# Seven block products instead of eight in both FFN products of the last six token chunks, with a new exchange of the turned probabilities and one load of queries and keys

## Chip, cores and metric

One core of one Trainium2 chip. The metric is the device time of one execution in microseconds (us); a kernel's time is the median of its runs.

## What is computed

Block-causal attention for 8 batches of 8 heads (576 positions, head dimension 64, blocks of 64 positions), then on its output, taken as 4608 tokens of 512 features, a feed-forward network (FFN) of two products with a leaky ReLU between them:

```python
scores = (1.0 / np.sqrt(D)) * np.matmul(q, k.transpose(0, 1, 3, 2))
scores = np.where(block_i >= block_j, scores, -1000000000.0)
attn = np.exp(scores - np.max(scores, axis=-1, keepdims=True))
attn = attn / (np.sum(attn, axis=-1, keepdims=True) + 1e-09)
attn_out = np.matmul(attn, v).astype(np.float32)
x = np.ascontiguousarray(attn_out.transpose(0, 2, 1, 3)).reshape(B * S, H * D)
h = x @ w_in                       # 4608 x 512 by 512 x 2048
g = np.maximum(0.01 * h, h)
return (g @ w_out).astype(np.float32)   # 4608 x 2048 by 2048 x 512
```

## The kernel before

Every operation is handed to a planner (class `Plan`, line 69) with a cost, a rank and the keys that it reads and writes. Before anything is issued the planner plays all five engines forward with its own costs and writes out one fixed order for each engine; on the chip each engine works through its list and waits by semaphores. A binary operation from SBUF on VectorE is marked "DVE+" (line 298): the planner never lets it run at the same time as an operation on GpSimd.

**FFN.** The tokens are cut into 18 chunks of 256 (`CH`). Every float32 operand is split into a high and a low part, and each product is the sum of three: high by high, high by low, low by high. A chunk has eight steps u. `ffn1` (line 845) makes two blocks of 128 rows of h from the chunk's x (`xh`, `xl`) in 24 matmuls of 256 columns (line 856); ScalarE applies the leaky ReLU (`g`, line 871), ScalarE or VectorE rounds it (`gh`), GpSimd as a rule subtracts (`gl`). `ffn2` (line 876) multiplies both blocks of g by `w_out` in 12 matmuls of 512 columns (line 883) into `p_o`, which collects over the eight steps; then ScalarE copies it to `ob` and it is stored. One chunk is 192 matmuls of 256 columns and 96 of 512. The core of both:

```python
terms = [((wih, wil)[w], x, d) for d in range(ND) for w, x in sides]
nc.tensor.matmul(p_h[z][:, i, :], w[:, d, f * P : (f + 1) * P], (xl if x else xh[y])[:, d, :], ...)
terms = [(a, w, i) for a, w in ((gh[z], woh), (gh[z], wol), (gl[z], woh)) for i in range(2)]
nc.tensor.matmul(p_o[m], a[:, i, m * P : (m + 1) * P], w[:, 2 * u + i, :], ...)
```

There is one `xl`: the low part of a chunk's x is written (`split_x`, line 821) when the chunk before has no first product left.

**Attention.** Heads 0 to 13 go one way. Heads 14 to 63 load queries and keys twice, into both halves of the partitions of `qk_in`, as one tile for query and key (line 509); both are scaled or rounded and their low parts subtracted (lines 511 to 521). After the softmax, VectorE transposes 32 x 32 squares of the probabilities (`turn`, line 749), and four DMAs write them to DRAM (`way`, line 774) and four read them back with their blocks exchanged (`ptm`, line 785); the product with the values reads `ptm` (line 680). The heads are spread over the FFN work of earlier batches; when the last head is done, only FFN chunks are left.

Of the kernel before, what the change touches and what calls it, by code (L numbers as in the profile page):

```python
# [9 lines left out]
F32 = mybir.dt.float32  # L10
# [26 lines left out]
RL = -2.566  # L37
RP = 4.143
RB = 0.5
RT = 2.976  # L40
RV = 0.818
RX = -0.204
RN = -1.299
RF = 4.338
PACE = [5.0, 5.0, 5.67, 5.0, 5.0, 5.0, 5.0, 5.0, 5.0, 5.0, 5.0, 5.0, 5.0, 5.0, 5.0, 5.0, 6.28, 5.0]
TWO = True
RM = -22.489

LEAD = 10.827
LAG = 1.995  # L50
RS = -17.449
RG = -4.487
OFF1 = 3.447
# [4 lines left out]
    "raw": (2200, 675), "first": (3300, 675), "v0": (1600, 900), "k": (900, 1170), "q": (500, 1110), "qk": (1500, 1325), "v": (450, 792),  # L58
    "way": (590, 385), "back": (1090, 1095), "out": (690, 354), "xs": (900, 400), "xin": (1500, 1100),
}  # L60
PADD = 2701.103
HOLD = 277.504
# [5 lines left out]
PAD = 595.177  # L68
PADO = 51.657
SPARE = 42.026  # L70
# [3 lines left out]
    [-0.34, -2.01, -1.04, -0.21, -0.2],  # L74
# [6 lines left out]
    [-0.3, 11.3, 1.53, -0.3, 0.55],  # L81
# [171 lines left out]

def act(n, sb=False):
    return n / 1.2 + (92 if sb else 52)
# [11 lines left out]
def attention_ffn(ctx: ExitStack, tc: tile.TileContext, q2: bass.AP, k2: bass.AP, qk: bass.AP, v: bass.AP, w_in: bass.AP, w_out: bass.AP, out: bass.AP):  # L267
# [38 lines left out]
    const = ctx.enter_context(tc.tile_pool(name="const", bufs=1))  # L306
    psum = ctx.enter_context(tc.tile_pool(name="psum", bufs=1, space=PSUM))
# [20 lines left out]
    way = fixed([4, P, 32 * slots], F32, "way", 2, dram)  # L328
# [13 lines left out]
    rows(0, const)  # L342
    qk_in = fixed([P, 2, S], F32, "qk_in")
# [7 lines left out]
    xr = fixed([P, ND, S], F32, "xr")  # L351
    xs = fixed([P, S], F32, "xs", 2)
    xin = fixed([P, ND, CH], F32, "xin")
    xt = [None] + fixed([ND, P, S], F32, "xt", B - 1, dram)
# [15 lines left out]
    g = fixed([P, 2, CH], F32, "g")  # L370
    gh = fixed([P, 2, CH], F32R, "gh", 2)
    gl = fixed([P, 2, CH], F32R, "gl", 2)
    xh = [fixed([P, ND, CH], F32R, "xh0")]
    xl = fixed([P, ND, CH], F32R, "xl")
    ob = fixed([P, DM], F32, "ob")

    early, coded = ExitStack(), ExitStack()
# [14 lines left out]
    def second_stage():  # L392
        coded.close()
        pool = ctx.enter_context(tc.tile_pool(name="late", bufs=1, side="right", reuse_waits="tile"))
        later["qs"] = fixed([P, S], F32R, "qs", 2, pool)
        later["ks"] = fixed([P, 2, S], F32R, "ks", None, pool)

    def third_stage():
        early.close()
        pool = ctx.enter_context(tc.tile_pool(name="last", bufs=1, reuse_waits="tile"))  # L400
# [580 lines left out]
```

## Time and profile before

| | |
|---|---|
| median of 3 runs (lowest, highest) | 1084.79 us (1084.07, 1092.26) |
| the profiled execution: its own time | 1086.14 us |
| its span, first to last instruction | 1084.4 us |

The difference of 1.7 us between the profiled execution's time and its span lies around the span. In the profile PE is TensorE's matmuls, DVE VectorE, ACT ScalarE, POOL GpSimd, SP the queue that issues all DMAs. A busy time counts a matmul from its issue until its results are out, and these overlap, so how fast TensorE works is read from the distance of starts.

### The profile page before, as it was taken

To read this page: it belongs to the slowest core of one execution; us is meant where nothing else is said; L and a number is where in the kernel's file an instruction comes from. 1 tells how busy PE (TensorE), PEld (TensorE's weight loads), DVE (VectorE), ACT (ScalarE), POOL (GpSimd) and SP (SyncE) were. 2 spreads that over 40 slices of the span, in tenths; PEclk is the share of its full clock that TensorE was granted. 3 is DMA by queue.
4 is the path that set the end of the run, shared out by engine and by line. 5 is a ranking of instruction groups with operands and counts; after the bars stand their busy time and mean duration, and the time that the engine had idled before them with its cause. 6 is when DMAs were issued, how large, how long until landed. Compare 5 with 4: busy or idle time off the path is not lost.

```text
span 1084.4 us, 19280 instructions
## 1 busy us (share of the span) xinstructions
PE 1055.5 (97%) x7048; PEld 913.8 (84%) x7048; DVE 562.5 (52%) x1564; ACT 525.8 (48%) x1297; POOL 326.2 (30%) x315
## 2 busy tenths in 40 slices
PE   7889999989999999999999999999999999999998
PEld 5658889878888889888888888888999999999997
DVE  7989878777787778676778776830000000000000
ACT  7787655655665556565555645632222222222222
POOL 3443334332332233323333332222222222222221
PEclk9989999999999999999999999999999999999999
DMA  7555427888999999887989979980101101001000
GB/s 208 176 173 158 150 97 222 240 255 244 304 247 258 270 250 299 249 248 229 266 245 259 297 229 270 268 222 21 41 5 36 39 1 40 20 20 40 1 21 20
DMA packets 107294, 179.86 MB, mean 166 GB/s; under 512 B 11968, under 2 KB 88768, under 8 KB 107200
## 3 DMA queue, kind: packets, MB, share of 16 engines
q1 hardware_dynamic: 107200, 178.63, 57.0%
q8 instruction: 56, 0.92, 0.4%
q14 instruction: 38, 0.31, 0.1%
HBM read 115.02 MB, written 63.57 MB: 165 GB/s over the span
## 4 chain that ended last, share of the span: by engine, by line
PE 73%; DMA 15%; DVE 5%; ACT 3%; issue 2%; SPq 1%; POOL 0%; ACTq 0%; POOLq 0%; DVEq 0%
PE p_o L883 29%; PE p_h L856 29%; DMA qk_in<-in_qk 8%; PE p_v L680 4%; DMA ptm<-way 3%; PE p_s L530 3%; PE p_v L541 2%; PE p_s L541 2%; PE p_v L636 1%; DMA way<-turn 1%; ACT prow L571 1%; DMA out<-ob 1%; DVE turn L760 1%; DVE nmrec L562 1%; PE p_v L724 1%
## 5 line engine op out<-in xcount | busy, mean ns | idle before, releaser
L298 POOL TENSOR_TENSOR gl<-g,gh 128x512 fp32r<-128x512 f32 x137 | 180.8, 1320 | 461.3 <-ACT gh L283 363.8
L856 PE MATMUL p_h<-xh,wih 128*128 128x256 f32 x1152 | 317.0, 280 | 0.0
L856 PE MATMUL p_h<-xh,wil 128*128 128x256 f32 x1152 | 314.5, 278 | 0.0
L856 PE MATMUL p_h<-xl,wih 128*128 128x256 f32 x1152 | 299.6, 278 | 0.0
L856 PEld LDWEIGHTS p_h<-xh,wih 128*128 128x128 f32 x1152 | 217.1, 188 | 9.5 <-issue 0.8
L871 ACT ACTIVATE g<-p_h 128x512 f32<-128x512 f32 x144 | 85.7, 595 | 281.3 <-PE p_h L856 276.8
L856 PEld LDWEIGHTS p_h<-xh,wil 128*128 128x128 f32 x1152 | 217.2, 189 | 0.6
L856 PEld LDWEIGHTS p_h<-xl,wih 128*128 128x128 f32 x1152 | 208.3, 189 | 8.4
L883 PE MATMUL p_o<-woh,gh 128*128 128x512 f32 x576 | 180.3, 394 | 1.4 <-ACT ob L283 1.2
L883 PE MATMUL p_o<-woh,gl 128*128 128x512 f32 x576 | 179.4, 393 | 0.2 <-POOL gl L298 0.2
L883 PE MATMUL p_o<-wol,gh 128*128 128x512 f32 x576 | 179.0, 392 | 0.0
L297 DVE TENSOR_TENSOR xl<-xin,xh 128x1024 fp32r<-128x1024 f32 (+3 forms) x21 | 19.5, 942 | 259.0 <-PE p_h L856 259.0
L760 DVE STREAM_TRANSPOSE turn<-prow 128x128 f32<-128x128 f32 (+3 forms) x400 | 144.4, 397 | 17.7 <-POOL prow L601 12.1
L883 PEld LDWEIGHTS p_o<-woh,gl 128*128 128x128 f32 x576 | 108.1, 188 | 24.6 <-POOL gl L298 0.7
L883 PEld LDWEIGHTS p_o<-wol,gh 128*128 128x128 f32 x576 | 108.2, 188 | 23.2
L601 POOL TENSOR_SCALAR prow<-prow,nmrec 128x448 f32<-128x448 f32 (+3 forms) x94 | 61.5, 660 | 196.6 <-DVE nmrec L588 150.2
L571 ACT ACTIVATE prow<-p_s,nmrec 128x320 f32<-128x320 f32 (+4 forms) x150 | 82.7, 558 | 41.7 <-DVE nmrec L562 40.1
L883 PEld LDWEIGHTS p_o<-woh,gh 128*128 128x128 f32 x576 | 90.4, 188 | 6.4 <-ACT ob L283 1.4
L571 ACT ACTIVATE prow<-p_v,nmrec 128x576 f32<-128x576 f32 (+1 forms) x150 | 71.2, 484 | 22.2 <-DVE nmrec L562 21.0
L283 ACT CAST gh<-g 128x512 fp32r<-128x512 f32 x126 | 78.1, 620 | 6.2 <-PE p_o L883 3.2
L680 PE MATMUL p_v<-ptm,vt 128*64 128x256 f32 (+3 forms) x700 | 78.7, 368 | 0.7 <-ACT prow L571 0.6
L562 DVE TENSOR_REDUCE nmrec<-p_s 128x1 f32<-128x448 f32 (+4 forms) x150 | 72.1, 520 | 1.4
(103 smaller groups left out, 1146.4 us busy)
## 6 DMA issues: line engine op xcount, KB each, us to landing
way<-turn SPq DMA_DIRECT2D x200, 224.0 KB, 4.7
ptm<-way SPq DMA_DIRECT2D x200, 224.0 KB, 6.0
qk_in<-in_qk SPq DMA_DIRECT2D x50, 576.0 KB, 4.9
out<-ob SPq DMA_DIRECT2D x35, 256.0 KB, 2.0
raw<-in_w_in SPq DMA_DIRECT2D x16, 512.0 KB, 4.1
raw<-in_w_out SPq DMA_DIRECT2D x16, 512.0 KB, 3.9
xt<-xs SPq DMA_DIRECT2D x28, 288.0 KB, 5.7
vt<-in_v SPq DMA_DIRECT2D x50, 160.0 KB, 5.9
```

The source lines that it names most:

```text
L283: one = lambda: nc.scalar.copy(dst(), src())
L298: ("POOL", pool2(n), lambda: nc.gpsimd.tensor_sub(dst(), one(), two())),
L530: go = lambda ap=ap, cols=cols, k0=k0, k1=k1, first=first, last=last: nc.tensor.matmul(ap, q_of()[:, cols], kt()[:, k0:k1], start=first, s ...
L541: nc.tensor.matmul(ap, later["qs"][z][:, cols], moving, start=first, stop=last)
L562: [("DVE", dve(kw[t]), lambda t=t, ap=ap, flat=flat: nc.vector.tensor_reduce(nm[z][: qn[t], at_col[t] : at_col[t] + 1], ap[: qn[t]], axis= ...
L571: nc.scalar.activation(o, ap[: qn[t]], AF.Exp, bias=nm[z][: qn[t], at_col[t] : at_col[t] + 1], scale=1.0, accum_out=sums[z][: qn[t], at_co ...
L601: ("POOL", pool1(kw[t]), lambda: nc.gpsimd.tensor_scalar(p(), p(), by, 1.0, op0=ALU.mult, op1=ALU.mult)),
L680: nc.tensor.matmul(dst, later["vt"][z][:, j], src, start=start, stop=stop)
L760: nc.vector.transpose(dst, src.rearrange("p (s b i) -> p s b i", b=4, i=32))
L856: nc.tensor.matmul(p_h[z][:, i, :], w[:, d, f * P : (f + 1) * P], (xl if x else xh[y])[:, d, :], start=first and k == 0 and (u > 0 or i == ...
L871: add([("ACT", act(512), lambda: nc.scalar.activation(g, p_h[z], AF.Prelu, alpha=0.01))], rank, [("h", z)], ["g"])
L883: nc.tensor.matmul(p_o[m], a[:, i, m * P : (m + 1) * P], w[:, 2 * u + i, :], start=u == 0 and k == 0, stop=u == NU - 1 and k == 5,)
```

## The change

1. **Tail.** The last six chunks are taken as three pairs of 512 tokens (`TAIL = 3`). In both FFN products each operand is seen as 2 x 2 blocks, and the product is made from seven products of blocks or of sums of blocks in place of eight, and additions of the results (a form of Strassen's scheme). `combos` makes the sums of blocks of `w_in`, and `combos2` those of `w_out`, from high plus low parts, and splits them again; `splits8` does it for x. `first8` runs a step of first products (42 matmuls), sums the results out of PSUM, applies the leaky ReLU and stores g in DRAM (`gd`); all 24 such steps come first. `second8` loads g, makes its sums and its high and low parts, and runs a step of second products (42 matmuls of 256 columns); 24 such steps come last. `combos` for seven of the eight steps uses the tile `xin` for its intermediate sums, so it starts when the last ordinary chunk has split its x. The columns of a step are now u and u + 8, and not 2u and 2u + 1.
2. **Turned probabilities.** Three DMAs write the blocks off the diagonal (12 of 16) to DRAM, six read them back into the same tile `turn`; four such tiles take turns.
3. **Queries and keys** are loaded once (64 partitions each of one tile, two tiles); the rounded key is written to both halves by two copies, and the low key by two subtractions, of 64 x 576.
4. **Planner.** Ranks and paces have new numbers. Binary operations of the tail (`op2`) are marked "DVE" and not "DVE+", so the planner lets them run beside GpSimd. `xh`, `xl`, `gh`, `gl` become parts of one tile `big`, and `g` and `ob` of one tile `piles`.

```diff
-PACE = [5.0, 5.0, 5.67, 5.0, 5.0, ...
+PACE = [5.0, 5.0, 5.67, 4.14, 5.0, ...
...
+def dve2(n):
+    return n / 0.96 + 110
...
-            add([("SP", ISSUE, lambda: nc.sync.dma_start(qk_in, qk[i - PLAIN]))], r0 - RL, [], ["qkt"], lag="qk")
+            add([("SP", ISSUE, lambda: nc.sync.dma_start(qk_in[:, z], qk[i - PLAIN]))], r0 - RL, [], [("qkt", z)], lag="qk")
...
+            for y in (1, 0):
+                half = slice(D * y, D * y + D)
+                add(subtracting(S, lambda half=half: kld()[half], k_of, lambda: khd()[D:]), rp, raw + [("kh", 1)], [("kl", y)])
...
+        for y, (a0, a1, b0, b1) in enumerate(((0, 1, 1, 4), (1, 3, 0, 4), (3, 4, 0, 3))):
...
+        for y, (b, a0, a1) in enumerate(((0, 1, 4), (1, 0, 1), (1, 2, 4), (2, 0, 2), (2, 3, 4), (3, 0, 3))):
...
-                    p_o[m], a[:, i, m * P : (m + 1) * P], w[:, 2 * u + i, :],
+                    p_o[m], a[:, i, m * P : (m + 1) * P], w[:, u + NU * i, :],
...
+        def op2(n, dst, one, two, plus, rank, reads, writes, by=None):
+            name = "tensor_add" if plus else "tensor_sub"
+            both = [
+                ("DVE", dve2(n), lambda: getattr(nc.vector, name)(dst(), one(), two())),
+                ("POOL", pool2(n), lambda: getattr(nc.gpsimd, name)(dst(), one(), two())),
+            ]
+            add(both[1:] if by == "POOL" else both, rank, reads, writes)
...
+        def split(n, top, low, src, rank, reads, tops, lows):
+            casting(n, top, src, rank, reads, tops)
+            op2(n, low, src, lambda: f32(top()), False, rank, reads + tops[:1], lows)
...
+        def combos(u, rank):
+            w0, w1 = wkeys[("wi", u)], wkeys[("wi", u + NU)]
+            s0, s1 = [("S", u, 0)], [("S", u, 1)]
+            heap, keys = (flat8, x8s) if u >= EARLY else (raw8, xins)
...
+            op2(CH, lambda: at(3), lambda: at(0), lambda: at(3), True, rank, [], keys)
...
+            split(3 * CH, lambda: sum8(u, 0), lambda: sum8(u, 1), lambda: at(1, 3), rank, keys, s0, s1)
...
+        def splits8(k, rank):
...
+            temp = lambda: xin[:, :2]
+            op2(WIDE, lambda: block(0, 1), lambda: block(0, 1), lambda: block(0, 0), False, rank, b11, b12)
+            op2(WIDE, temp, lambda: block(1, 1), lambda: block(0, 1), False, rank, b22 + b12, ["xa"])
...
+        def first8(k, u, rank):
...
+                terms = [(d, w, 0) for d in range(2) for w in range(2)] + [(d, 0, 1) for d in range(2)]
...
+                    nc.tensor.matmul(
+                        bank()[:, :CH], stationary(j, u, w, d), operand(j, x)[:, d],
+                        start=j not in (4, 6) and n == 0, stop=n == 5, skip_group_check=j in (4, 6),
+                    )
...
+        def second8(n, rank):
...
+            op2(CH, lambda: cells(3, 4), lambda: cells(2, 3), lambda: cells(0, 1), False, rank + RS8, [near[0], near[2]], [near[3]])
...
+                terms = [(x, 0, w) for x in range(2) for w in range(2)] + [(x, 1, 0) for x in range(2)]
...
+                    nc.tensor.matmul(
+                        to(), operand(j, low)[0][:, x * P : (x + 1) * P], moving(j, us[x], w),
+                        start=q == 0 and m == 0 and j in opens, stop=q == 3 and m == 5 and (spot[j][1] == 1 or j == 2),
+                    )
```

How the lists of TensorE and VectorE read at the two places of which the prediction speaks. First TensorE near the end of the kernel before, in its last chunk: line 856 is the first product, line 883 the second.

```order
L856 MATMUL p_h1_704<-xh0_112,wih_63 128x256
L856 MATMUL p_h1_704<-xl_113,wih_63 128x256
L856 MATMUL p_h1_704<-xh0_112,wil_64 128x256
L883 MATMUL p_o1_102<-woh_65,gh1_109 128x512 x2
L883 MATMUL p_o1_102<-wol_66,gh1_109 128x512 x2
L883 MATMUL p_o1_102<-woh_65,gl1_111 128x512 x2
```

And TensorE in the changed kernel where its last ordinary chunk (the twelfth) goes over into the tail: line 921 is the ordinary second product, line 1092 the block products; `new_8057` and `big_106` hold the parts of x and of g, `sum8_0_8060` the split sums of the weights of step 0. Ahead of these rows stand the ordinary chunk's last first product and two block products, into `p_s` (from `new_8057`) and `p_v` (from `big_106`).

```order
L1092 MATMUL p_h1_690<-new_8057,wih_63 128x256
L1092 MATMUL p_h1_690<-new_8057,wil_64 128x256
L1092 MATMUL p_h1_690<-new_8057,wih_63 128x256
L1092 MATMUL p_h1_690<-new_8057,wil_64 128x256
L1092 MATMUL p_h1_690<-new_8057,wih_63 128x256 x2
L921 MATMUL p_o0_100<-woh_65,big_106 128x512 x2
L921 MATMUL p_o0_100<-wol_66,big_106 128x512 x2
L921 MATMUL p_o0_100<-woh_65,big_106 128x512 x2
L921 MATMUL p_o1_101<-woh_65,big_106 128x512 x2
L921 MATMUL p_o1_101<-wol_66,big_106 128x512 x2
L921 MATMUL p_o1_101<-woh_65,big_106 128x512 x2
L1092 MATMUL p_s_98<-new_8057,sum8_0_8060 128x256 x6
```

Three block products now stand ahead of the chunk's last second product; from the fourth on there is nothing but the tail in TensorE's list.

VectorE in the last five rows of the kernel before, which split x of the last chunks:

```order
L297 TENSOR_TENSOR xl_113<-xin_91,xh0_112 128x4x64
L284 CAST xh1_1479<-xin_91 128x1024
L297 TENSOR_TENSOR xl_113<-xin_91,xh1_1479 128x1024
L284 CAST xh0_112<-xin_91 128x1024
L297 TENSOR_TENSOR xl_113<-xin_91,xh0_112 128x1024
```

And VectorE in the changed kernel beside the last ordinary chunk: the seventh `combos` (sums in `xin_79`, then `wih_63` and `wil_64`), behind it the parts of x for the tail (`big_106`, `new_8057`), line 965 being `op2` on VectorE.

```order
L965 TENSOR_TENSOR xin_79<-wih_63,wil_64 128x512
L965 TENSOR_TENSOR xin_79<-wih_63,wil_64 128x256 x2
L965 TENSOR_TENSOR xin_79<-xin_79 128x256 x4
L298 CAST wih_63<-xin_79 128x2x128
L298 CAST big_106<-x8_8058 128x512
L965 TENSOR_TENSOR wil_64<-xin_79,wih_63 128x2x128
L965 TENSOR_TENSOR big_106<-x8_8058,big_106 128x512 x2
L311 TENSOR_TENSOR big_106<-piles_107,big_106 128x512
L965 TENSOR_TENSOR xin_79<-x8_8058 128x512
L965 TENSOR_TENSOR x8_8058<-xin_79,x8_8058 128x2x256
L965 TENSOR_TENSOR new_8057<-xin_79,new_8057 128x512
L965 TENSOR_TENSOR new_8057<-x8_8058,new_8057 128x512
```

Where VectorE had single rows with long pauses between them, it now has a chain of seven such groups; the part of x that the second block product reads (`big_106` from `x8_8058`) stands behind the last group's sums, and the parts made with `xin_79` as an intermediate, which the fourth block product reads, behind that.

## Rows read from the trace of the kernel before

**Rows 1.** Busy time by engine; the span in 40 slices (tenths): matmuls, VectorE, granted clock.

```profile
PE 1055.5 (97%) x7048; PEld 913.8 (84%) x7048; DVE 562.5 (52%) x1564; ACT 525.8 (48%) x1297; POOL 326.2 (30%) x315
...
PE   7889999989999999999999999999999999999998
...
DVE  7989878777787778676778776830000000000000
...
PEclk9989999999999999999999999999999999999999
```

**Rows 2.** Two stretches: PE, PEld, DVE, ACT, POOL busy; clock, DMA share, GB/s.

```profile
100.00:700.00 600.00, 590.29 (x4014) 508.57 (x4013) 451.03 (x1286) 348.24 (x912) 197.23 (x192) 1.00 0.85 244
800.00:1050.00 250.00, 250.00 (x1635) 227.83 (x1634) 11.25 (x14) 62.73 (x104) 59.45 (x46) 1.00 0.07 24
```

**Rows 3.** The chain that ended last: start us, us, engine, tile, line, instructions.

```profile
744.10 1.37 PE p_o L883 x6
...
753.75 1.39 PE p_h L856 x12
...
767.55 2.75 PE p_h L856 x24
...
1032.32 2.75 PE p_h L856 x24
```

**Rows 4.** Groups of VectorE instructions by form: count, busy us, mean ns of one.

```profile
L297 DVE TENSOR_TENSOR ks<-qk_in,ks 128x576 fp32r<-128x576 f32 x28 | 22.1, 790 | 2.3 <-ACT ks L283 1.7
...
L297 DVE TENSOR_TENSOR xl<-xin,xh 128x1024 fp32r<-128x1024 f32 x10 | 12.1, 1210 | 153.6 <-PE p_h L856 153.6
...
L297 DVE TENSOR_TENSOR gl<-g,gh 128x512 fp32r<-128x512 f32 x7 | 4.8, 688 | 0.8 <-ACT gh L283 0.8
L297 DVE TENSOR_TENSOR xl<-xin,xh 128x768 fp32r<-128x768 f32 x4 | 3.8, 946 | 39.5 <-PE p_h L856 39.5
...
L739 DVE TENSOR_TENSOR xr<-p_o,xr 128x512 f32<-128x512 f32 x2 | 1.4, 688 | 0.2 <-ACT xr L283 0.2
...
L297 DVE TENSOR_TENSOR xl<-xin,xh 128x256 fp32r<-128x256 f32 x3 | 1.2, 407 | 29.5 <-PE p_h L856 29.5
```

**Rows 5.** Groups on GpSimd (the first in 800 to 1050 us) and ScalarE.

```profile
L298 POOL TENSOR_TENSOR gl<-g,gh 128x512 fp32r<-128x512 f32 x46 | 59.5, 1292 | 193.2 <-ACT gh L283 193.2
...
L298 POOL TENSOR_TENSOR ks<-qk_in,ks 128x576 fp32r<-128x576 f32 x22 | 31.8, 1446 | 15.6 <-ACT ks L283 11.1 <-ACT qs L286 1.8 <-DMA out<-ob 1.4
...
L283 ACT CAST gh<-g 128x512 fp32r<-128x512 f32 x126 | 78.1, 620 | 6.2 <-PE p_o L883 3.2
```

**Rows 6.** The timeline of VectorE and GpSimd at two moments: start us, us.

```profile
179.59 1.79 POOL L298 TENSOR_TENSOR gl<-g,gh 128x512 fp32r<-128x512 f32 x1
...
180.26 1.74 DVE L297 TENSOR_TENSOR ks<-qk_in,ks 128x576 fp32r<-128x576 f32 x1
...
657.46 1.21 DVE L297 TENSOR_TENSOR xl<-xin,xh 128x1024 fp32r<-128x1024 f32 x1
...
657.68 2.14 POOL L298 TENSOR_TENSOR gl<-g,gh 128x512 fp32r<-128x512 f32 x1 [0.43 <-DVE gh L284]
```

**Rows 7.** Two stretches about the fall of the clock (columns of rows 2).

```profile
72.00:75.60 3.60, 1.60 (x13) 1.12 (x11) 3.23 (x8) 2.45 (x5) 1.08 (x1) 1.00 0.82 266
75.60:82.60 7.00, 5.85 (x20) 4.88 (x21) 3.44 (x9) 4.71 (x11) 2.88 (x2) 0.51 0.30 91
```

**Rows 8.** DMA issues: count, KB each, median us from issue to landing.

```profile
way<-turn SPq DMA_DIRECT2D x200, 224.0 KB, 4.7
ptm<-way SPq DMA_DIRECT2D x200, 224.0 KB, 6.0
qk_in<-in_qk SPq DMA_DIRECT2D x50, 576.0 KB, 4.9
```

**Rows 9.** What TensorE waited for, longest first: us in total, times, longest us.

```profile
PE p_s L530 <- ACT k_in L286: 4.6, 1, 4.6
PE p_v L636 <- ACT prow L571: 3.1, 2, 1.8
PE p_s L541 <- POOL ks L298: 2.6, 2, 2.5
```

More of the change, by code (lines that the diff above doesn't have):

```diff
@@ L57 @@
 MOVES = {
-    "raw": (2200, 675), "first": (3300, 675), "v0": (1600, 900), "k": (900, 1170), "q": (500, 1110), "qk": (1500, 1325), "v": (450, 792),
-    "way": (590, 385), "back": (1090, 1095), "out": (690, 354), "xs": (900, 400), "xin": (1500, 1100),
-}
-PADD = 2701.103
-HOLD = 277.504
[3 rows of a table added]
+}
+PADD = 4400.167
+HOLD = 266.733
 FILL = 235
@@ L366, in narrow @@
         p_h.extend(fixed([P, 2, CH], F32, "p_h", 2, pool=pool))
[L370 to L377, printed above, removed]
+    big = fixed([P, 4, ND, CH], F32R, "big")
+    xh, xl = [big[:, 0]], big[:, 1]
+    gh, gl = ([big[:, 2 + y, 2 * x : 2 * x + 2] for y in range(2)] for x in range(2))
+    piles = fixed([P, 2, DM], F32, "piles")
+    g, ob = piles[:, 0].rearrange("p (a b) -> p a b", a=2), piles[:, 1]
+    tied, early, coded, late = ExitStack(), ExitStack(), ExitStack(), ExitStack()
+    pool = tied.enter_context(tc.tile_pool(name="tied", bufs=1, reuse_waits="tile"))
+    rows(0, pool)
+    qk_in = fixed([P, 2, S], F32, "qk_in", None, pool)
+    xr = fixed([P, ND, S], F32, "xr", None, pool)
+    xs = fixed([P, S], F32, "xs", 2, pool)
     pool = early.enter_context(tc.tile_pool(name="early", bufs=1, reuse_waits="tile"))
@@ L399, in third_stage, with fourth_stage @@
         early.close()
-        pool = ctx.enter_context(tc.tile_pool(name="last", bufs=1, reuse_waits="tile"))
-        later["ptm"] = fixed([P, turned], F32, "ptm", 2, pool)
-        later["turn"] = fixed([P, turned], F32, "turn", 2, pool)
+        pool = early.enter_context(tc.tile_pool(name="last", bufs=1, reuse_waits="tile"))
+        later["turn"] = fixed([P, turned], F32, "turn", TURNS, pool)
         later["vt"] = fixed([P, NT, D], F32, "vt", 2, pool)
         xh.append(fixed([P, ND, CH], F32R, "xh1", None, pool))
+    def fourth_stage():
+        for stack in (late, early, tied):
+            stack.close()
+        pool = ctx.enter_context(tc.tile_pool(name="tail", bufs=1, reuse_waits="tile"))
+        later["new"] = fixed([P, 3, ND, CH], F32R, "new", None, pool)
+        later["x8"] = fixed([P, ND, WIDE], F32, "x8", None, pool)
+        later["more"] = fixed([P, 3 * CH + 80], F32, "more", None, pool)
+        later["sum8"] = [fixed([P, 2, 3, CH], F32R, f"sum8_{u}", None, pool) for u in range(NU)]
     def weight_piece(num, rank, f, out_side, c0):
@@ L760, in go @@
                 nc.vector.transpose(dst, src.rearrange("p (s b i) -> p s b i", b=4, i=32))
-            add([("DVE", dve(k * P), go)], r0 + RT, pkeys(t), [("turn", z, t, j)] + ([("turn", z, 4, 4)] if t == 0 else []))
+            add([("DVE", dve(k * P), go)], r0 + RT, pkeys(t), [("turn", x, t, j)] + ([("turn", x, 4, 4)] if t == 0 else []))
         flipped(1, 3, 8, 4, 0, k=2)
@@ L904, in attention_ffn @@
+    pieces = [(u + NU * i, o, c) for u in range(NU) for i in range(2) for o in (False, True) for c in range(0, DM, WIDE)]
     wkeys = {}
@@ L943, in attention_ffn @@
                 ffn2(c, u, rank + rate[c] * LAG / NU + 0.003)
+    tail()
     if FILL:
```

395 lines of the change are left out of this document (332 added, 63 removed), and 3 rows, old and new, of the table MOVES.

## The prediction

> **What bounds the kernel now.** I read the summary of busy times and slices first, then two stretches, then the chain that ended last, then the waits. Matmuls are in flight 97% of the span, and from slice 28 on VectorE stands still while TensorE goes on at the full clock [rows 1]: attention is over, only FFN chunks are left. From 800 to 1050 us TensorE has no gap at all, with VectorE busy 11 us of 250 and the DMA engines 7% [rows 2]. So the stage that the change rewrites is bound by how many columns TensorE streams. From 100 to 700 us, where the heads are interleaved with chunks, TensorE is busy 590.3 of 600 us [rows 2]: all waits on attention together cost 9.7 us there. The DMA engines are 85% busy in that stage [rows 2], but what TensorE waits for in the whole trace are single waits of ScalarE and GpSimd results, 4.6 us at the longest [rows 9].
>
> **TensorE's work.** The chain shows a chunk starting every (1032.32 - 767.55) / 6 = 44.13 us [rows 3]. A chunk is 192 matmuls of 256 columns and 96 of 512, that is 384 units of 256 columns: 0.1149 us a unit. The last six chunks are 264.8 us. Afterwards they are 24 steps of 42 first products and 24 steps of 42 second products, 2016 units: 231.7 us. That removes 33.1 us. The sum needs one thing more: the second products now run 256 columns wide, so there are 1008 instructions (each with its weight load) for 576. In the chain 12 matmuls of 256 columns take 1.39 us and 6 of 512 take 1.37 us [rows 3]; a unit costs the same either way, so I add nothing.
>
> The Trainium skill (TensorE: Matmul & The Clock Gate, Back-to-back issue gap) speaks against this edit: it gives 81 ns a matmul at 128 columns and 131 ns at 512 in a sustained stream, by which (an estimate on the straight line between) two of 256 would cost 196 ns in place of 131. By that rule the second products would become 23 us longer and not 16.6 us shorter, and the kernel would come out near 1102 us. The rows above it, 116 ns and 229 ns, show no fixed cost per matmul for these operands, so I give it no weight.
>
> **What the other engines must do for it.** VectorE and GpSimd were nearly free in that stage; the change gives them sums and splits. Rows 6 show what this costs when both read two SBUF operands: GpSimd's `gl`, 1.29 us when undisturbed [rows 5], began 0.2 us behind a VectorE subtraction and took 2.14 us, so it ran only after that had ended; and VectorE's `ks`, 0.79 us on average [rows 4], began inside a `gl` and took 1.74 us. Such operations exclude each other, and the one that comes second waits. The planner of before knows this ("DVE+"); for the tail's operations it has been told that they may run together. So its order is tighter than the chip, and I add up the two engines' times where they share a deadline. Durations are those of rows 4 and 5: on VectorE 0.407, 0.688, 0.946 and 1.21 us for 256, 512, 768 and 1024 columns (a sum with a PSUM operand takes the same, 688 ns at 512); on GpSimd 1.29 us for 512 and, in proportion, 0.65 for 256 and 1.9 for 768. No row has GpSimd at those two widths.
>
> *The way into the tail.* The seven `combos` cannot start before the last ordinary chunk's low part of x is written, 1.7 us after that chunk's first matmul (0.95 + 0.41 us and the wait), and the second block product, which needs a part of x queued behind them, stands 402 units = 46.2 us after that matmul; a cast, two subtractions and a wait, 1.7 us, come between. That leaves 42.8 us. VectorE has 9 operations of 512, 45 of 256, 6 of 768 columns and 5 casts of about 0.3 us to do: 6.2 + 18.3 + 5.7 + 1.4 = 31.6 us; GpSimd has 8 `gl` and 3 of 256: 12.3 us. Together 43.9 us. The chain also stops seven times for ScalarE's cast of 768 columns (620 ns at 512 [rows 5]), some 0.4 us each beyond what VectorE does meanwhile, 3 us in all. If the engines never met, 34.6 us would fit and nothing is lost; with every meeting and every stop in full it is some 49 us and TensorE stands for 6 us, with only block products queued behind the one that waits. I take 4.
>
> *First-product steps (115.8 us).* VectorE has 120 sums out of PSUM, 48.8 us, and 66 operations on SBUF (23 of 512, 34 of 256, 8 of 768, 1 of 1024), 38.4 us, with some casts 89 us. GpSimd has 51 us. Without meetings both fit: 0. If VectorE did nothing while GpSimd works: 89 + 51 - 116 = 24 us. In between, 66 operations each find GpSimd busy with a chance of 51 / 116 and wait half of its mean 0.87 us: 12.6 us more, VectorE busy 102 of 116 us. It is an in-order queue, so the sums that free PSUM banks are late when an operation ahead of them waits. The nearest row is the stretch 100 to 700 us, where VectorE was busy 75% and TensorE lost 1.6% [rows 2], 2 us here; with VectorE at 88% I take 5.
>
> *Second-product steps (115.8 us).* VectorE: 72 operations on SBUF, 58.0 us, and 42 sums, 17.1 us; GpSimd 32 us. Even added up, 107 us, they fit, and VectorE's share, 65%, is below that of the row just named: I take 2, from 0 to 10.
>
> *DMA.* The tail writes and reads g (24 x 0.66 MB each way) and the sums of `w_out` (3.1 MB each way), 38 MB in 232 us, 163 GB/s, where 244 GB/s went through in 100 to 700 us [rows 2]. A load is issued about two steps ahead, 9.7 us; loads of 576 KB landed in 4.9 us with the queues full [rows 8]. Hidden; if that cover goes, a step waits for its g, which is within the 10 us above. The end is as before but for a VectorE sum in place of a ScalarE copy: nothing.
>
> **The attention edits.** Queries and keys halve 576 KB a head, and the exchange drops a quarter of 4 x 224 KB each way [rows 8]: 37 MB less of DMA. But those transfers lie beside FFN matmuls, and no wait of TensorE on them is among the longest [rows 9]; the most that could come back is the 9.7 us of rows 2. Against it stand 50 more copies (about 0.62 us) and 50 more subtractions (0.79 us on VectorE or 1.45 on GpSimd [rows 4, 5]), 70 to 104 us spread over three engines that were busy 451, 348 and 197 of 600 us [rows 2], and one more DMA issue a head. They lie beside FFN matmuls too; without that cover the 9.7 us might double. From -9 to +10; I take 0.
>
> **Sum.** Against the profiled execution: 1086.1 - 33.1 + 4 + 5 + 2 = 1064.0 us. Its own time lies 1.35 us above the median of the runs, so I forecast 1063 us for the median.
>
> **Rivals.** *The gain comes whole.* The engines rarely meet, and the order has slack that I do not see: 1086.1 - 33.1 - 1.35 = 1052 us. For it: VectorE's shares of 65 to 77% in the tail are no higher than in 100 to 700 us, where 98.4% of TensorE's time was used [rows 2]. Against it: the two measured meetings [rows 6] and the 43.9 us of work for 42.8.
>
> *The clock falls at the way in.* In 72.0 to 75.6 us TensorE was busy 1.6 of 3.6 us, and for the 7 us after that the granted clock was 0.51, 1.2 in place of 2.4 GHz [rows 7]: half of 7 us, 3.5 us, are lost each time. A stand of 4 us before the block products could bring one such fall: 1066 to 1067 us, still inside my forecast; falls in the first-product steps as well would make it 1072 or more.
>
> *The shared access to SBUF becomes the bound (the other side).* If every operation of VectorE, its PSUM sums too because they queue in order, waits while GpSimd works, the bounds above add up: 6 + 24 + 10 = 40 us, more than the 33.1 saved, and the kernel takes 1092 us, slower than before. It decides from the point where the first-product steps take 24 us longer than their matmuls. For it: in-order queues and PSUM banks (five of eight are held per step) that turn a late sum into a stop. Against it: a sum reads one SBUF operand only, and the trace has VectorE's 451 us beside GpSimd's 197 us in 600 us at a loss of 9.7 us [rows 2].
>
> *The attention edits take back part.* +10 us on the forecast: 1073 us.
>
> **How the numbers follow.** The forecast, 1057 to 1072 us, has a chance of 0.50; the whole gain or better, under 1057, 0.24; a larger part given back, by clock falls, the attention stage or longer steps, 1072 to 1086 us, 0.17; the shared access as bound, over 1086, 0.09. A measurement tells about 1% from no change: under 1074 is faster, over 1095.6 slower. Faster has 0.50 + 0.24 and a little of the third, 0.76; slower half of the last, 0.05; within 1% the rest, 0.19. The range runs from the whole gain with some of the attention's 9.7 us (1050) to where the last rival begins (1086).
>
> **What would show it.** In the changed kernel's profile: matmul starts of the tail 0.115 us apart in both products (else the unit price is wrong); a wait of TensorE of some 4 us at the second block product, on VectorE or ScalarE, some 46 us after the last ordinary chunk began; GpSimd and VectorE operations of the tail longer than their rows here, in pairs; small waits, some 5 us in all, in the first-product steps and fewer in the second; 100 to 700 us with TensorE busy 580 to 600 us. A time near 1052 us with VectorE's operations at their undisturbed lengths would refute the shared access; a TensorE that waits all through the tail, or a clock row with several falls, would refute the size of my middle terms.

## The result and the profile after

The changed kernel takes 1071.36 us (median of 4 runs, 1070.62 to 1071.98), the kernel before beside it 1085.76 us; the ratio is 0.9856, 95% interval 0.9814 to 0.9898. It is 1.4% faster, as forecast in sign and within the range of 1050 to 1086 us, and 8 us slower than the forecast of 1063 us. The gain, however, does not come from where the prediction put it.

From the page of the changed kernel: its span, the busy time of TensorE and VectorE, and of the 40 slices the rows of matmuls, VectorE and granted clock.

```profile
span 1070.2 us, 21248 instructions
...
PE 1027.7 (96%) x7336; PEld 910.8 (85%) x7336; DVE 798.8 (75%) x1932; ACT 610.5 (57%) x1437; POOL 420.1 (39%) x413
...
PE   7979999999999999999999999999999789889998
...
DVE  7887978688778787878768778760998767578664
...
PEclk9999999999999999999999999999999999999999
```

Before, TensorE's row held nines to the end [rows 1]; now it breaks in the slices 31 to 35 (counted from 0), about 830 to 960 us, in which VectorE is at 5 to 8 tenths where it stood still before.

The stretches of the changed kernel (time, then busy us of PE, PEld, DVE, ACT, POOL; clock, DMA share, GB/s):

```profile
100.00:700.00 600.00, 600.00 (x4121) 521.90 (x4120) 469.37 (x1294) 393.29 (x980) 240.57 (x238) 1.00 0.65 193
700.00:790.00 90.00, 90.00 (x606) 80.00 (x605) 52.60 (x106) 34.89 (x69) 25.16 (x20) 1.00 0.34 102
790.00:810.00 20.00, 20.00 (x143) 18.72 (x142) 17.36 (x34) 9.19 (x18) 6.77 (x6) 1.00 0.18 60
810.00:935.00 125.00, 109.79 (x907) 106.18 (x906) 88.68 (x168) 50.04 (x114) 56.15 (x54) 1.00 0.59 179
935.00:955.00 20.00, 14.63 (x101) 13.55 (x100) 14.30 (x17) 6.67 (x9) 9.34 (x7) 0.91 0.69 211
955.00:1065.00 110.00, 108.05 (x911) 107.23 (x909) 74.96 (x102) 39.95 (x46) 42.05 (x40) 1.00 0.45 141
```

Two things stand against the prediction's sum. From 100 to 700 us TensorE shows no pause, and it issues 4121 matmuls where it issued 4014 [rows 2]. And in the tail, from 810 us on, it pauses for 15.2, 5.4 and 2.0 us.

To place the tail's start, matmuls by line, with the first and last start (us): the last second products of the kernel before, then of the changed kernel the last ordinary second products, the first block products, and the last.

```profile
L883 PE MATMUL p_o<-woh,gl x576: 388/392/502, 95.0 to 1080.2; 128*128 128x512 f32 x192
```

```profile
L921 PE MATMUL p_o<-woh,big x768: 387/392/636, 91.7 to 800.2; 128*128 128x512 f32 x192
...
L1092 PE MATMUL p_s<-new,wih x48: 275/277/388, 795.6 to 927.3; 128*128 128x256 f32 x48
...
L1221 PE MATMUL p_o<-woh,new x48: 279/280/281, 965.9 to 1065.6; 128*128 128x256 f32 x48
```

Before, the work of six chunks, 264.8 us by the prediction's price, ends at 1080.4 us, so it begins at 815.6 us. Now the ordinary chunks end at 800.4 us, and 18 matmuls of block products (2.1 us, from 795.6 us on) have already been issued between their last matmuls: the tail begins, in units of work, at 798.3 us. **Everything ahead of the tail became 17.3 us shorter; the tail, to 1065.7 us, takes 267.4 us in place of 264.8, 2.6 us longer;** the stores after the last matmul take 0.5 us more. -17.3 + 2.6 + 0.5 = -14.2 us, the difference of the spans, 1084.4 and 1070.2. The seven products saved 33.1 us of columns, and the tail gave all of it back.

How they gave it back, in the changed kernel's chain that ended last (start us, us, what):

```profile
905.86 1.36 PE p_o L1092 x12
...
922.30 3.85 DMA gd<-more
...
928.12 3.96 DMA gd<-piles
...
933.52 3.61 DMA sum<-td
...
938.38 0.98 PE p_v L1221 x6
...
944.95 2.42 DVE x L965 x2
...
954.72 1.41 PE p_v L1221 x12
```

Between the first and the second products the chain leaves TensorE: stores of g, the block sums of `w_out` coming back from DRAM, and VectorE's splits stand in it. VectorE's groups between 796 and 930 us (count, busy us, mean ns of one):

```profile
L965 DVE TENSOR_TENSOR x<-x 128x256 f32<-128x256 f32 x28 | 19.2, 687 | 0.0
...
L965 DVE TENSOR_TENSOR x<-woh,wol 128x512 f32<-128x512 f32 x6 | 6.4, 1072 | 1.0 <-DMA td<-x 1.0
L1105 DVE TENSOR_TENSOR piles<-piles,p_v 128x256 f32<-128x256 f32 x15 | 6.3, 418 | 5.5 <-PE p_v L1092 2.7 <-ACT piles L297 2.5
```

Operations with two SBUF operands take 687 ns at 256 columns and 1072 at 512, where 407 and 688 are undisturbed [rows 4]; the sums with a PSUM operand keep their 418 ns. And two moments of the timeline (start us, us, and in brackets how long the engine stood before and for what):

```profile
874.66 0.37 ACT L297 COPY piles<-p_s 128x256 f32<-128x256 f32 x1 [1.44 <-DMA gd<-piles]
...
875.55 0.39 PE L1092 MATMUL p_v<-new,wih 128*128 128x256 f32 x1 [2.04 <-DVE piles L1105]
...
879.88 0.69 DVE L965 TENSOR_TENSOR x<-x 128x512 f32<-128x512 f32 x1 [2.92 <-DMA x<-xt]
...
880.96 0.97 PE L1092 MATMUL p_h<-big,sum 128*128 128x256 f32 x6 [1.73 <-DVE piles L1105]
```

In the first, ScalarE may not write a pile again until its store has landed, and the sums behind it free no PSUM bank. In the second, VectorE stands at the head of its queue behind the load of the third pair's x (its buffer had served the sums of `w_out` until then), while finished sums wait behind it. TensorE is named as waiting for a sum both times.

### The profile page after: what moved, and what is told of

It reads as the page before. It is cut to its first block, busy times and chain, and to the rows that moved or that the text cites. A ratio compares the mean times of both kernels' runs of the same rounds, so it can differ in the third digit from the quotient of the medians.

```text
span 1070.2 us, 21248 instructions
## 1 busy us (share of the span) xinstructions
PE 1027.7 (96%) x7336; PEld 910.8 (85%) x7336; DVE 798.8 (75%) x1932; ACT 610.5 (57%) x1437; POOL 420.1 (39%) x413
## 5 line engine op out<-in xcount | busy, mean ns | idle before, releaser
L894 PE MATMUL p_h<-big,wih 128*128 128x256 f32 x1216 | 246.7, 281 | 0.0
L921 PE MATMUL p_o<-woh,big 128*128 128x512 f32 x768 | 236.8, 395 | 0.0
L894 PEld LDWEIGHTS p_h<-big,wih 128*128 128x128 f32 x1216 | 200.0, 189 | 10.0 <-issue 2.2
L312 POOL TENSOR_TENSOR big<-piles,big 128x512 fp32r<-128x512 f32 x80 | 106.3, 1329 | 204.0 <-ACT big L297 169.6
L921 PEld LDWEIGHTS p_o<-woh,big 128*128 128x128 f32 x768 | 133.3, 188 | 21.4 <-issue 2.4
L894 PE MATMUL p_h<-big,wil 128*128 128x256 f32 x448 | 123.4, 280 | 0.0
L921 PE MATMUL p_o<-wol,big 128*128 128x512 f32 x384 | 119.7, 393 | 0.0
L894 PE MATMUL p_h<-xh,wih 128*128 128x256 f32 x320 | 87.8, 280 | 0.0
L894 PE MATMUL p_h<-xh,wil 128*128 128x256 f32 x320 | 87.3, 278 | 0.0
L894 PEld LDWEIGHTS p_h<-big,wil 128*128 128x128 f32 x448 | 85.2, 190 | 0.3
```

Source lines behind the costliest of these rows:

```text
L312: ("POOL", pool2(n), lambda: nc.gpsimd.tensor_sub(dst(), one(), two())),
```

## Experiments: what is ahead of the tail

Each ratio below is to the kernel before, run on the same chip beside it. The runs were made on several chips, and beside them the kernel before took 1082.1 to 1083.4 us, where it took 1085.76 beside the change; so runs on different chips are compared by their ratios or by their traces, not by their times alone.

**Attention edits without the tail.** The planner number `TAIL` makes the last six chunks ordinary again:

```diff
-TAIL = 3
+TAIL = 0
```

> The changed kernel with TAIL = 0: attention, its loads, its exchange and all new planner numbers as changed, but the last six chunks as ordinary chunks again. Theory A (the attention edits and the new order bring the last six chunks forward, the seven products save nothing): in the changed kernel's trace the first block product starts at 795.6 us; before, six chunks of 44.13 us ending with the last matmul at 1080.4 us begin at 815.6 us. So this kernel should take about 1085 - 20 = 1065 us, 6 us LESS than the changed kernel, with TensorE busy 600 of 600 us between 100 and 700 us. Theory B (as predicted: the attention edits are worth 0, the products bring the gain): 1085 us within 5. Between the two, 1075 us, would mean that the earlier start belongs half to the tail's freer planning.

Measured: 1068.56 us, ratio 0.9848 (0.9807 to 0.9889), the same as the full change within the intervals. Its stretches:

```profile
100.00:700.00 600.00, 600.00 (x4116) 521.60 (x4115) 469.25 (x1292) 392.49 (x979) 240.50 (x237) 1.00 0.65 193
790.00:1060.00 270.00, 270.00 (x1759) 245.79 (x1758) 11.20 (x13) 67.57 (x112) 63.33 (x49) 1.00 0.07 22
```

The tail is again without a pause, with VectorE idle, as in [rows 2], and the whole gain is there: theory A. That theory had 1065 us; its 20 us counted the 2.75 us of ordinary matmuls that run among the first block products as tail.

**Which of the attention edits.** On this kernel one part after the other is put back; the cuts show the main lines of each. First, the loads, and with them the casts and subtractions of before:

```diff
-add([("SP", ISSUE, lambda: nc.sync.dma_start(qk_in[:, z], qk[i - PLAIN]))], r0 - RL, [], [("qkt", z)], lag="qk")
+add([("SP", ISSUE, lambda: nc.sync.dma_start(qk_in, qk[i - PLAIN]))], r0 - RL, [], [("qkt", 0)], lag="qk")
...
-qk = np.ascontiguousarray(np.concatenate([x[PLAIN:] for x in two], axis=1))
+qk = np.stack([x[PLAIN:] for x in two], axis=2)
+qk = np.ascontiguousarray(np.concatenate([qk, qk], axis=1))
```

> As e1_front_only, but queries and keys are loaded as before: 576 KB a head with both copied to the upper 64 partitions, one buffer, one cast of 128 partitions each, one subtraction for the keys. If the single load (half the bytes, two buffers, so the load is no longer waited for by the cast) brings the earlier start, this kernel loses it: some 10 to 20 us above e1_front_only, with ScalarE waiting for that load again (60 us in all before). If the exchange or the numbers bring it: within 3 us of e1_front_only, or even faster, since 50 copies and 50 subtractions go.

Measured: 1083.67 us, ratio 0.9999 (0.9974 to 1.0024): all of it is lost. Second, the exchange:

```diff
-TURNS = 4
+TURNS = 2
...
-dst = later["turn"][x][32 * b : 32 * b + 32, a0 * w : a1 * w]...
+dst = later["ptm"][x][32 * b : 32 * b + 32]...
```

> As e1_front_only, but the turned probabilities go out whole and come back whole into tiles of their own (4 stores and 4 loads of 224 KB a head, two buffers of each tile in place of four of one). If the exchange in one tile (a quarter of the bytes less, four heads deep) brings the earlier start: 10 to 20 us above e1_front_only, with TensorE again waiting between 100 and 700 us. If the loads or the numbers bring it: within 3 us of e1_front_only.

Measured: 1071.61 us, ratio 0.9877 (0.9834 to 0.9919): nearly all is kept, so the exchange in one tile earns little or nothing. Third, the planner's numbers, all but its estimates of DMA times:

```diff
-RL = -2.684
-RP = 2.849
-RB = -0.783
-RT = 1.737
+RL = -2.566
+RP = 4.143
+RB = 0.5
+RT = 2.976
...
-RM = 11.035
+RM = -22.489
...
```

> As e1_front_only, but with the planner's numbers of the kernel before (ranks, chunk pace, slack), only the DMA estimates stay new. If a better order alone brings the earlier start: about 1085 us, 20 above e1_front_only. If the loads and the exchange bring it whatever the order: within 5 us of e1_front_only. The numbers were fitted to other instructions, so a time above 1085 us would say only that they don't fit, not what the edits are worth.

Measured: 1084.18 us, ratio 1.0014 (0.9987 to 1.0041): without the new numbers the new loads earn nothing. (The numbers of before had been chosen for the instructions of before.) The same stretch in these three, in this order, one fence each:

```profile
100.00:700.00 600.00, 589.72 (x4015) 512.06 (x4014) 450.70 (x1287) 361.56 (x940) 201.65 (x195) 1.00 0.73 220
```

```profile
100.00:700.00 600.00, 599.47 (x4103) 521.22 (x4102) 464.10 (x1248) 378.85 (x940) 248.03 (x238) 1.00 0.75 213
```

```profile
100.00:700.00 600.00, 589.42 (x4016) 512.53 (x4017) 473.73 (x1280) 377.67 (x955) 253.25 (x243) 0.99 0.65 191
```

With the loads or the numbers of before, TensorE is back at some 590 us and 4015 matmuls; with the exchange of before it is not, although the DMA share rises to 0.75. So the bytes moved were not the limit by themselves.

**What in the loads.** Beside the new casts, two things changed there: half the bytes, and two buffers for one. This kernel keeps the casts and the halved bytes and takes the second buffer away:

```diff
-add([("SP", ISSUE, lambda: nc.sync.dma_start(qk_in[:, z], qk[i - PLAIN]))], r0 - RL, [], [("qkt", z)], lag="qk")
+add([("SP", ISSUE, lambda: nc.sync.dma_start(qk_in[:, 0], qk[i - PLAIN]))], r0 - RL, [], [("qkt", 0)], lag="qk")
...
```

> As e1_front_only, queries and keys still loaded once (288 KB a head, casts and subtractions as changed), but into one buffer in place of two alternating ones, as before. Theory P (the second buffer is what counts: with one, the load of a head's queries and keys can start only when the casts of the head before have read the last, so the casts of each head stand behind a DMA's landing time, 3.8 us or more): most of the earlier start is lost, 1076 to 1084 us, with ScalarE or VectorE waiting for that load again and TensorE under 598 of 600 us. Theory Q (the halved bytes and the shorter chain of casts count): 1067 to 1071 us, as e1_front_only.

Measured: 1089.81 us, ratio 1.0084 (1.0050 to 1.0117), slower by 0.8% than the kernel before. That is theory P's side, above its range of 1076 to 1084 us; why it is slower than the kernel with the loads of before, at the same wait (below), stays open. What ScalarE waited for between 100 and 700 us (us in total, times, longest us), first before, then with the loads put back, then with one buffer:

```profile
ACT qs L286 <- DMA qk_in<-in_qk: 60.2, 30, 4.7
```

```profile
ACT qs L300 <- DMA qk_in<-in_qk: 63.7, 27, 5.6
```

```profile
ACT qs L300 <- DMA qk_in<-in_qk: 63.9, 30, 5.9
```

In the changed kernel this wait is 1.7 us in all:

```profile
ACT qs L300 <- DMA qk_in<-in_qk: 1.7, 3, 0.8
```

With one buffer the next head's load starts only after this head's last cast, and ScalarE stands at the cast for 60 us in total; with two, the load has landed. With the numbers of before and two buffers that wait is small as well, 5.8 us, and yet nothing is gained: the gain needs the second buffer and the new numbers together. That the buffer makes the data early and the new ranks use it is the reading of this; which of the numbers does it was not tried, nor two buffers with the full bytes.

## Experiments: the tail

**A planner that knows of the exclusion.** One word in `op2`:

```diff
-("DVE", dve2(n), lambda: getattr(nc.vector, name)(dst(), one(), two())),
+("DVE+", dve2(n), lambda: getattr(nc.vector, name)(dst(), one(), two())),
```

> The changed kernel with one word changed: the tail's operations with two SBUF operands are marked DVE+ on VectorE, so the planner no longer lets them run beside GpSimd's. Theory X (the order is bad because the planner does not know the exclusion; VectorE's 256-column operations took 0.69 us where 0.41 is undisturbed): operations near their undisturbed lengths, TensorE's pauses between 796 and 950 us, some 32 us now, fall by 10 us or more: 1055 to 1062 us. Theory Y (VectorE simply has too much to do in those steps, in any order): the same waiting moves from inside the operations to between them: within 4 us of 1071.

Measured: 1078.96 us, ratio 0.9970 (0.9952 to 0.9988): slower than the change as it is. In its stretch of 800 to 930 us the operations did become shorter:

```profile
L965 DVE TENSOR_TENSOR x<-x 128x256 f32<-128x256 f32 x28 | 13.3, 492 | 0.5 <-POOL x L966 0.5
L965 DVE TENSOR_TENSOR x<-woh,wol 128x512 f32<-128x512 f32 x13 | 10.9, 864 | 1.5 <-DMA td<-x 1.4
```

492 ns for 687, but 13 of the sums of `w_out` run on VectorE in place of 6, and TensorE pauses longer, first of all at the way into the tail, where the change has no pause:

```profile
790.00:810.00 20.00, 16.38 (x100) 14.81 (x99) 16.87 (x36) 6.64 (x12) 0.00 (x0) 0.91 0.07 27
```

Theory X falls, and Y's "within 4 us" was missed as well. The prediction's remark that the order is "tighter than the chip" is true: operations do meet. But the plan that avoids the meetings also hands out the work otherwise, and as a whole it costs more than they do.

**The work taken out.** The loads and splits of the second and third pair (they multiply the first pair's operands instead) and the sums of `w_out`, left out together:

```diff
-            if k:
-                inputs8(k, TR + 8 * k - 2)
-                splits8(k, TR + 8 * k - 2)
...
-                        combos2(y, TR + SUMS[y])
-                if k == TAIL - 1:
-                    combos3(u, TR + 8 * k + u)
```

> The changed kernel without part of its work: the second and third pair of chunks multiply the first pair's operands (their loads and splits are left out), and the block sums of w_out are not made, stored or loaded. What stays in the first-product steps: all products, the sums out of PSUM, the leaky ReLUs, the stores. Theory Y (VectorE's load of operations on SBUF ahead of the sums that free PSUM banks holds TensorE up): the pauses of the first-product steps after the way in, some 22 us, fall under 6 and the step to the second products shrinks too: about 1045 us. Theory Z (the chain from product to sum to bank is itself too long, five banks a step): the pauses stay, 1065 us or more.

Measured: 1048.98 us, ratio 0.9702 (0.9680 to 0.9724). Theory Y, Z falls. Then each half alone, first without the loads and splits, then without the sums of `w_out`:

> One half of what e6_products_and_sums left out: the second and third pair of chunks multiply the first pair's operands (their loads from DRAM and their splits are left out); the block sums of w_out are made. The two halves together gave 1049 us. If the splits and the loads that they wait for hold TensorE up (VectorE stood 2.9 us at 877 us behind the load of the third pair's x, and TensorE paused at 847 to 855 and at 879 us): 1053 to 1060 us. If the block sums of w_out do: 1064 us or more.

Measured: 1063.98 us, ratio 0.9840 (0.9811 to 0.9870).

> The other half: the block sums of w_out are not made, stored or loaded (second products use what lies there), the splits of all pairs are made. If the block sums of w_out hold TensorE up, by VectorE's time and by the buffer that the next pair's load needs: 1053 to 1060 us, and the step to the second products, 8.5 us of pauses in 20 us, falls to about 3. If the splits do: 1064 us or more. If the two halves each give most of the 22 us, the cost lies in their meeting, not in either.

Measured: 1050.64 us, ratio 0.9717 (0.9681 to 0.9754). Against the 1071.36 us of the change, the splits and loads of the second and third pair are worth 7 us, the sums of `w_out` 21 us, both together 22. By the ratios it would be 2, 15 and 17 us, the first of them within the intervals. The traces bear the larger figures: reckoned as above, the tail takes 259.5, 245.9 and 244.8 us for 267.4, in one execution each. By either count most hangs on the sums of `w_out`. The stretches without these sums, cut at its own step from first to second products:

```profile
810.00:921.00 111.00, 107.88 (x915) 106.40 (x914) 63.34 (x134) 45.33 (x103) 28.37 (x30) 1.00 0.52 155
921.00:941.00 20.00, 18.08 (x151) 17.47 (x150) 14.46 (x18) 7.68 (x10) 6.76 (x7) 1.00 0.63 190
941.00:1045.00 104.00, 102.05 (x866) 101.23 (x865) 71.12 (x98) 37.91 (x44) 38.91 (x38) 1.00 0.46 143
```

Against the changed kernel's stretches, the pauses of TensorE are 3.1 us for 15.2 and 1.9 for 5.4. The same stretch of the first products without the splits, then without both:

```profile
810.00:925.00 115.00, 106.76 (x888) 103.77 (x887) 72.36 (x150) 42.02 (x98) 38.88 (x44) 1.00 0.57 173
```

```profile
810.00:917.00 107.00, 106.62 (x900) 105.26 (x900) 47.75 (x113) 37.13 (x89) 17.08 (x23) 1.00 0.46 140
```

With the change, without the splits, without the sums, without both, VectorE is busy 71, 63, 57 and 45% of this stretch, GpSimd 45, 34, 26 and 16%, and TensorE loses 12, 7, 3 and 0.4%: the loss falls in step with their work. With the sums also go their stores and loads and their use of the buffer of x, which these runs do not tell apart from the engines' time. The stores of g are all still there in the last kernel, so by themselves they do not hold TensorE up.

**The return of the sums.** They come back from DRAM behind the last first products, so the block products that need them were put last:

```diff
-order = (4, 5, 6, 0, 1, 2, 3) if q == 0
+order = (4, 6, 0, 3, 5, 1, 2) if q == 0
```

> The changed kernel with another order of the block products in the first two second-product steps of each pair: those that need no block sum of w_out (4, 6, 0, 3) first, then 5, 1, 2. TensorE stood 8 us between 930 and 953 us, where the block sums come back from DRAM behind the last first products (3.6 us a load, then a cast and a subtraction). If that return holds it: the later need (three products, 2.1 us) takes 2 to 4 us off: 1067 to 1069 us. If the splits of g hold it, which stand in the same place: within 1.5 us of 1071.

Measured: 1072.86 us, ratio 0.9918 (0.9890 to 0.9946): no gain, and 5.5 us of pauses from 935 to 955 us as before (5.4), so this return alone does not hold the step.

**Another place for the sums.**

```diff
-SUMS = [1, 2, 4, 10, 11, 12, 14, 19]
+SUMS = [1, 2, 4, 16, 17, 18, 19, 20]
```

> The changed kernel with one row of numbers changed: five of the eight block sums of w_out move from the steps 10, 11, 12, 14, 19 to 16, 17, 18, 19, 20, behind the last pair's splits, so that the last pair's load no longer waits for the buffer that these sums use. Theory H (what holds TensorE in the steps 8 to 15 is VectorE standing at the head of its queue behind that load, and the crowd of sums and splits in the same steps): the pauses from 847 to 881 us, some 10 us, shrink by more than come after 890 us: 1064 to 1068 us. Theory Y (VectorE has too much to do in any order): the pauses move to the steps 16 to 20, within 2 us of 1071.

Measured: 1064.92 us, ratio 0.9849 (0.9817 to 0.9882). And between the two:

```diff
-SUMS = [1, 2, 4, 10, 11, 12, 14, 19]
+SUMS = [1, 2, 4, 9, 10, 18, 19, 20]
```

> The changed kernel with the block sums of w_out at the steps 1, 2, 4, 9, 10, 18, 19, 20: two between the second pair's splits and the third pair's load, three behind the third pair's splits. In e11_sums_late (1065 us, five of them at 16 to 20) VectorE was busy only 9.7 of 20 us from 850 to 870, and TensorE paused 10 us from 885 to 925, where sums and splits met; in the changed kernel it was the other way round. Theory H (the place of these sums decides, because they meet the splits, the loads that need their buffer, and the stores): pauses of the first-product steps under 20 us, 1060 to 1065 us. Theory Y (VectorE has too much to do in any order): within 3 us of the e11 kernel, the pauses merely elsewhere.

Measured: 1068.38 us, ratio 0.9868 (0.9838 to 0.9898). The pauses move: with the late sums TensorE is busy 112.37 us of 124 up to its second products, 11.6 us lost, and VectorE stands behind the loads of x for 2.9 us where it stood 4.8, but 18.42 of 20 us of VectorE and 16.42 of GpSimd are taken from 890 to 910 us, where sums and splits now meet.

```profile
810.00:934.00 124.00, 112.37 (x919) 109.03 (x918) 89.57 (x173) 52.42 (x117) 56.63 (x52) 0.99 0.60 185
...
890.00:910.00 20.00, 18.04 (x150) 17.25 (x149) 18.42 (x33) 9.20 (x20) 16.42 (x15) 1.00 0.65 200
```

All three places lie in one another's intervals. By time the late sums lie in theory H's range, by ratio they are the change; the kernel between the two misses the ranges of both theories. In the traces the tail takes 261.4 us with the late sums and 266.0 between the two, for 267.4: so a few us may hang on the place (theory H) but not the 20 us. What fits these runs and those with work taken out is that the amount of work in these steps decides, as theory Y has it. None of the kernels that compute everything is measurably faster than the changed kernel: 0.9848 without the seven products, 0.9849 with the late sums, 0.9856 as it is.

## Why the prediction was right in sign and wrong in its steps

**TensorE's columns, -33.1 us: right.** A unit costs what the chain said, almost: 12 matmuls of block products take 1.36 us in one stretch and 1.41 in another, all second products 1.41, that is 0.1178 for 0.1149, 2.9 us over 1008. The 1008 second products take 118.7 us, where 576 of 512 columns took 131.5 (1.37 us for 6 [rows 3]). The rule of the Trainium skill (TensorE: Matmul & The Clock Gate, Back-to-back issue gap), weighed in the prediction, by which (its estimate) the second products would become 23 us longer, does not hold here: the measurement decides.

**The way into the tail, +4: measured 0.** From 790 to 810 us TensorE is busy 20.00 of 20, but the margin was small. GpSimd's last write of the sums that the second block product reads, and that product (start us, us):

```profile
793.38 2.24 POOL L966 TENSOR_TENSOR sum<-xin,sum 128x768 fp32r<-128x768 f32 x1 [3.07 <-DVE wil L965]
...
796.34 0.84 PE L1092 MATMUL p_v<-big,sum 128*128 128x256 f32 x6
```

The sums were ready at 795.62 us, at most 0.7 us ahead. The 43.9 us of work in 42.8 us were an upper bound treated as the likely value. (With the 3 us of stops it adds up to 46.9 us, not to "some 49", so the bound was 4 us of standing and not 6.) With the meetings planned away the same place does lose 3.6 us (above).

**First-product steps, +5 (0 to 24), second-product steps, +2 (0 to 10): the size failed.** The tail takes 267.4 us, 35.7 above its 231.7 of columns, where 4 + 5 + 2 = 11 were given. The stretches show 15.2 us of it in the first-product steps, 5.4 at the step to the second products and 2.0 after. Counted from start to start of the matmuls, which also finds what the view of busy times hides (below), the trace has 20.9, 8.5 and 3.0 us there beyond the price of a unit, the fall of the clock included; with some 3 us for the dearer unit that is the whole 35.7. So the first-product steps (798.3 to 934.9 us) lost 20.8 us, inside the range given, and the second-product steps (to 1065.7 us) 15.0, outside it. The step that failed is the choice of the row: "The nearest row is the stretch 100 to 700 us, where VectorE was busy 75% and TensorE lost 1.6%". VectorE's amount was forecast well: it was busy 98 us in the first-product steps, where 102 were forecast, waiting for GpSimd included in both. What such a share costs TensorE was not. There a late result holds up one head while chunks fill TensorE's queue. In the tail every block product needs a PSUM bank that a sum in the same queue must free, and nothing else is there to issue: at 71% of VectorE TensorE lost 12%, and with the sums of `w_out` gone, at 57%, 3%. The mechanism named ("the sums that free PSUM banks are late when an operation ahead of them waits") is what the timeline shows; the upper bounds, 24 and 10, come nearer to what was measured.

**DMA "hidden": not wholly.** A pile waits for its store (1.44 us at 874 us), VectorE for the third pair's load (2.92 us at 879 us), the second products for g and the sums of `w_out`. The estimate weighed bandwidth; what these waits show is the time to landing of a store or load whose buffer is needed next. What they cost by themselves no run shows; with the sums and splits taken out and all stores of g left, TensorE loses 0.4%.

**The attention edits, 0 (-9 to +10): measured -17.3, outside its bounds.** The sentence that failed is "the most that could come back is the 9.7 us of rows 2". It fails in two ways. First, the view: a group of the kernel before between 100 and 700 us (count, busy us, mean ns of one) is

```profile
L856 PE MATMUL p_h<-xh,wih 128*128 128x256 f32 x600 | 164.9, 280 | 0.0
```

A matmul is on record for 280 ns, and the next starts 116 ns after it began [rows 3]. A pause shorter than 164 ns leaves no gap, and each longer one is shown 164 ns too short. The count of matmuls tells the truth: 107 more in the same 600 us are 107 * 600 / 4121 = 15.6 us (by columns, 77 more matmuls of 256, 37 more of 512 and 7 fewer of attention's, 16.6 us). Second, the argument that no wait of TensorE on those transfers is among the longest [rows 9] looked at the last link only. ScalarE's 60.2 us behind the load stood in the trace of before, and so did the load itself, with 8% of the span, in the chain that ended last. The shares of that chain by line, first before, then with the attention edits alone (e1_front_only), where the load has gone from it (`in_q` is that of the first heads):

```profile
PE p_o L883 29%; PE p_h L856 29%; DMA qk_in<-in_qk 8%; PE p_v L680 4%; DMA ptm<-way 3%; PE p_s L530 3%; PE p_v L541 2%; PE p_s L541 2%; PE p_v L636 1%; DMA way<-turn 1%; ACT prow L571 1%; DMA out<-ob 1%; DVE turn L760 1%; DVE nmrec L562 1%; PE p_v L724 1%
```

```profile
PE p_h L894 38%; PE p_o L921 37%; PE p_v L710 7%; PE p_v L570 4%; PE p_s L570 3%; PE p_s L559 2%; PE p_v L665 1%; PE p_v L754 1%; PE p_w L559 1%; ACT prow L600 0%; DMA raw<-in_w_in 0%; PE p_o L665 0%; ACT ptf L297 0%; DMA qk_in<-in_q 0%; DMA raw<-in_w_out 0%
```

TensorE's own waits carried other names (ScalarE, VectorE and GpSimd results). The load is not the whole account: with the numbers of before its wait is nearly gone too, and nothing is gained.

**Rivals.** "The gain comes whole" and "the shared access becomes the bound" were both too simple: the tail did give the whole saving back, much as the second had priced it (34 us in its steps), by sums that queue in VectorE's order; that every operation meets another was not needed for it (the plan without meetings is slower still). And the time is lower only since the attention edits gained what no case held. The clock fell once in the tail (below). That the sign came out right is luck: it rests on two errors of opposite sign, +25 us in the tail and -17 us ahead of it, which leave 8 us between forecast and result. With the error in the tail alone the kernel would have come out near 1088 us, above the kernel before.

## What to carry to other kernels

Saved columns count only where the engines that must prepare and collect have slack in the same steps; price the added work step by step against the bank or buffer that it frees, and take the upper bound where nothing else can fill the wait. Bound what an edit can give back by the number of instructions issued in a stretch, not by the idle time of an engine whose records overlap. Look at waits two links back, and at the chain that ended last: putting the single-buffered load back cost 15 us here (1083.67 for 1068.56, on one chip), and no wait of TensorE between 100 and 700 us is longer than 2.0 us in that kernel.

## What the runs showed of the hardware

The same block product of 256 columns starts 113 ns or 118 ns after the one before it (1.36 and 1.41 us for 12, in the chain); in the changed kernel's chain nearly all second products run at the slower pace. What decides it stays open.

TensorE's clock fell at the step to the second products:

```profile
935.20:938.40 3.20, 0.86 (x6) 0.45 (x5) 2.94 (x5) 1.19 (x3) 0.28 (x1) 1.00 1.00 312
938.40:942.00 3.60, 3.60 (x22) 3.60 (x23) 0.76 (x2) 0.87 (x2) 2.29 (x3) 0.68 0.85 251
```

It was busy 0.86 of 3.2 us, and in the 3.6 us that followed the granted clock was 0.68 on average, partly at 1.2 in place of 2.4 GHz: here the pause was paid for twice, as at the start of the kernel before [rows 7]. And VectorE's and GpSimd's operations with two SBUF operands lengthen each other as [rows 6] had it, VectorE's by 0.28 us at 256 columns and 0.38 at 512 on average, GpSimd's sums of `w_out` at 512 columns to 1591 ns for 1292 [rows 5], while sums with a PSUM operand keep their 418 ns.
